# Turning the softmax weights of 320 queries by DMA instead of on TensorE, in a fused attention and Mish MLP kernel

## The chip, the cores and the metric

The kernel runs on one core of a Trainium2 chip. The metric is the device time of one execution, in microseconds. The engines are named as in the profile: PE is TensorE (PEld its weight loads), DVE is VectorE, ACT is ScalarE, POOL is GpSimd, SP is SyncE, which here only issues DMAs.

## The reference, cut to what matters

```python
B, H, S, D = 4, 8, 576, 64                 # batch, heads, queries, head size
q_rot, k_rot = rotate(q), rotate(k)
scores = (1 / sqrt(D)) * q_rot @ k_rot.T
attn = exp(scores - max(scores)); attn = attn / (sum(attn) + 1e-9)
x = (attn @ v)                             # as rows of 8 heads * 64 = 512, 2304 tokens
h = x @ w_in                               # 512 -> 2048
g = h * tanh(log1p(exp(min(h, 20))))       # Mish
out = g @ w_out                            # 2048 -> 512
```

All inputs are fp32. The kernel keeps their accuracy by holding a number as a pair of fp16 values (a high part and the rest), and multiplying pairs in three matmuls: high by high, high by rest, rest by high.

## The kernel before

Two heads make a pair, and four pairs make a batch, so there are 16 pairs, `P` from 0 to 15. Each pair has its 576 queries in steps `step(P, t)`: four steps of 128 queries (`t` 0 to 3), and one step `t` = 4 that takes the last 64 queries of two pairs together. A step is: scores on PE (L505), the maximum on DVE (L513), exp with its sum on ACT (L515), and 1 / sum on DVE (L523, L525). The weights that come out have queries on the partitions, and must be turned, so that keys stand there, before they can be multiplied with V. The turned weights of the first 256 queries of a pair (`k` = 0, steps 0 and 1) and of its last 320 (`k` = 1, steps 2 to 4) go into one tile `et` each, and one call `av(P, k)` multiplies each with V. There are two ways to turn them:

- The exact way keeps fp32. PE transposes the 128 by 128 blocks (L549, L564), sends 1 / sum through a matmul too (L566), ACT or DVE copy the blocks from PSUM to `et` (L558, L559, L573, L575) and 1 / sum to `ew` (L577, L579). `av` is nine fp32 matmuls per half (L636 to L639), and DVE then multiplies with 1 / sum (L667).
- The fp16 way scales the weights to a pair of fp16 values in `ew`: the high part on POOL, ACT or DVE (L530, L532, L533), the rest on DVE (L537). SP issues one DMA transpose for a step (L623), and `av` is 27 fp16 matmuls (L644, L648, L649). V must be there as an fp16 pair, which `cast_v` makes (a load L463, then L466 to L470).

Either way `av` ends with the two halves of `xt`, the fp16 pair of x: its high part (L670, L672) and its rest on DVE (L675). Which way is taken stands in one function, for batch 0 alone:

```python
def exact(P, k):
    return P < NP and (k == 0 or P < NX)
...
    own = exact(P, int(t > 1))
...
    if own:
        turned(es, [(st["ET", p, k], at, t, st["R", p, k], q) for p, k, at, q in to], r)
        return
```

`NP` is 4. The MLP works on 8 blocks of tokens, `c` from 0 to 7: block 2b holds the first 256 queries of batch b, block 2b + 1 its last 320. `h_unit` multiplies with w_in (L883) and takes Mish on ACT (L888), `h_split` makes fp16 pairs (L898, L899, L902), `p_sub` multiplies with w_out (L919). Both weights come as fp32 and are made into fp16 pairs by `decode` (L761 to L781), which needs their largest exponent first: a maximum on DVE (L728), two tiny matmuls on PE and tiny operations on DVE between (L336 to L355). w_out comes in four parts; the loads are L715.

Nothing is scheduled at run time. All operations are recorded in a plan, and the table `ORDER` says in which order they are issued: each entry is an operation's number, with a letter for the engine that takes it where there is a choice, `@` for its PSUM bank, and `+n` for n matmuls without use (L1034, function `fill`) put before it on PE. Every engine works through its own instructions in that order.

Of the kernel before, what the change touches and what calls it, by code (L numbers as in the profile page):

```python
# [50 lines left out]
NX = 2  # L51
# [14 lines left out]
    202 138 105@2 458 162 229@3 184 106 189 34 164 192@2 146 193b 148 144 147 194 208 233 37 185 44 93 35 190 234
    153@1+13 149 165@0 47 51 166 41 235 195 154 236@0 214@54 251b 150 237 49 459 303b 155@1 238 230 209 196 239 107@2
    215 297b 240@0 151 217 216 203 241 152 218 167 285 157@3+6 191 245b 357 270@54 315b 286 158 197 109 108 156 242
    273 159 337@0+5 244@2 48 271 356 250@1 530 219 246 52 274 168 220 287 243 272 247 288@3 252 50 248 169@2 280@4 221
    275 338 53 460 289 170 606 224@0 290 253 257 54 222@3 291 281 276 55 378 292@2 225 322@54 223 293 377 56 256@1  # L70
    278@0 263 581b 462 226@2 277 325 249 279 323 326 282@3 379 461 394 324 380@0 283 294 258 610 341@45+4 228 227 254
    172 381 463 284 339 330@2 296@0 342 373@3 615 331 529 344 231 343 298 259 345 613 299 349@2 262@4 374 332@1 309
    328 260 464 346 327 351@0 347 382 329 350 264 465@3 333 348 383 466 384@2 352 340 353@1 385 375 265 334@3 314@0
    232 266 376 358@54 316 336 267 355 335 386 354 467 302@2 317 454@3 359 308@1 412 468 361 360 400 310 261 362 387
    469@0 311 318 418@54 255 389 455 390 304 456 607 366@1 470 457 305 319 526@3 367 421 411@0 406 171 419 422 546@2
    611 413 420 210 183 414 527 368@4 364 391 423 635@1 212 312b 369b 424 415b 393@5 666@0 268 363 416 471 211 547 395
    636 604@3 396 405@2 619 667 407 399@4 698@1 616 425 408 605 664 401 428@0 409 402 426@3 696 365 269 665 435@54 429
    300b 397 549 370@2 699 398 438 427 783@0 436 439 403b 410b 681@1 371b 404 434 372b 437 800@3 697 433 682 550 612
    511@45 759 472 301 801 818@2 512 57 798 614 755 514 784 430@1 313 641 819 756 760 440 443@3 515 432b 441 822@0 442
    617 445b 431b 213 444b 505 474 446@2 620 513 449@1 499c 447 700 531@54 452 799 306 517 448 388 307 450b 295 820  # L80
    451b 600@3 532 453 826 534 644 533 320 473 535 487 823 516 642 475 536 321 518 476@2 392 523@5 477 757 417 601
    519@1 493 701 478 479 539@2 525b 524b 643 520b 618 480@3 824@4 702 481 482 608b 483 540 537 827 907@0 504@1 821
    825 506 609 498@3 873@5 871 507 908 500 521@2 874 645 501 541@1 602 522 587@45 713 872 542 508b 911 538 603 543@0
    588 509 492@3 830@2 502 545b 544b 494 486@1 503 660@0 495 589 484 590 528 912 637 496b 591 488 497 831 592 717
    622@45 593 575 594 661 489 595 828@3 662 623 703 596b 625 1087@0 829 548 626 743 714 1102 485 551 663 510 598
    552@2 624 553 597 490 646@54+5 638 554 491 628 627 555 629 761 630b 556@1 647 711 1103 631 749b 599 649 648 557
    633 650 632 909 668@54+5 652 651 558 653 559 910 574@3 669 654 634 1130 639 576 655 670 656 1131 568@2 1133@1+5
    657 569b 577 640 658 1147 671 578 570 672 563 571 704 580@0 683@54+4 579 715 572 674 673 562@3 582 1148 573 712
    718 1132 675 564 659 677b 676 780@2 684 705 686 685 565 621 687 583 1175 708 716 566 688 781 719 567b 584 720@3
    721 709 1176 689 560 722 1177 723 690 706 782 724@0 692b 767@54 725 726 679 727 832 737b 1178@3 691b 678 730@1 768  # L90
    731 680 1192 585 770 769 732 771 694 707 785@54 742@2 693 733 835 695 1193 786 734 788 787 735 1232 744 789 772
    790 745 833 748@0 802@54 773 791 561 736@1 774 728 586 750 1233 834 738 746 1235@2 751 776b 836 792 739 775b 815@3
    963 778 740 794b 741b 793b 747b 1249 777 752 850 1234 805 710 1250 753b 806 803 964 875 816 1274 879 817 804 779
    795 837@45 808 854 807 729 809 810b 936@0 838 876 811 754 1275 796 0 877 913@1 881 840 965 839 797 841 966 842 880
    957@3 914 843 812 857@45 844 851 883 845b 915@2 958 860 967 937 846b 813 1036 917@1 916 882 878 861 858 951@3 847
    991 848 859 934 884 1037 894@54 952 862 1276 885 863 953 1039 932@0 1314 864 895 866b 814 897 896 1038 981@2 898
    935 1 918 899 1040 886@3 919@54 1194 887 852 888 849 889 933 868 961@3 983 922 855 959 900 995 1041 1011@1 962 987
    865b 960 985@0 901 996 920 1012 982 903c 902b 867 1030@3 853 984 869 986 921 1032b 890@1 905 1034@2 891 870 1013b
    893 923 1014 1059@0 1031 924 925 904 1042b 938@54 926 1033 1060 954@1 1035 939 928 988 1083b 927b 1195b 940 1084
    1015@3 906 941 992 892 1063@0 942 943 930 1016 929 968@54 764 1196b 931 944 1197 945 946b 1081@2 969 1064 947b  # L100
    1061b 1277@3 971 993 1082 1327 989 949 1108 972 1294 1062 948 1295 970 990 974 950 955b 1085 973 975 998@45 977b
    1086 1315 979 1310 976b 1001 1109 997 999 1002 1078@0 978 1311 1000 1328 1111 980 1017@54 1207 1003 1079b 1004
    1112 1005 1007b 1313@2 1018 1006 856 1020 1019 1104 1110 1149 956 1021 1009 1331 1043@54 1080 1008 1022 1023
    1056@3 1024 1046 1026b 1044 1047 1025c 1312 1028 1355 1045 1010 1105b 1209 1027 1106 1065@45 1113 1049 1107 1048
    1050 1332 1051b 1356 1029 1057 1066 1052b 1150 1058 1067 1068 1370 994 1070 763 1054 1069 1316 1198 1071 1088@45
# [993 lines left out]
```

## Time and profile before

| | us |
|---|---|
| median of 3 runs | 617.98 (616.5 to 618.74) |
| the profiled execution | 618.88 |
| its span in the trace | 616.8 |
| PE busy | 591.1 (96%) |
| DVE busy | 458.0 (74%) |
| ACT busy | 392.1 (64%) |
| POOL busy | 249.5 (40%) |

Busy time is the time in which an engine executes at least one instruction. The fill matmuls count as busy time of PE. The profiled execution took 0.9 us longer than the median.

### The profile page before, as it was taken

Reading aid. Unit: us, or ns where it says so; the run is one execution under the profiler, and the core shown is the slowest. Engines: PE = TensorE matmul, PEld = TensorE weight load, DVE = VectorE, ACT = ScalarE, POOL = GpSimd, SP = SyncE. Lnnn points to the kernel's source line nnn. Section 1 sums busy time; section 2 is a strip of 40 time slices with the busy share of each in tenths; the row PEclk is TensorE's granted clock in tenths of the full one; section 3 lists DMA queues with packets and bytes.
Section 4 is the critical chain, followed back from the end, with each engine's and each line's share of the span. In section 5 each row is a group of like instructions: output and inputs, shape, how many; then the busy total and the mean of one; then the engine's idle time right before and its main releaser. Section 6 shows DMA issues by size and latency. Waiting matters only on the chain.

```text
span 616.8 us, 12860 instructions
## 1 busy us (share of the span) xinstructions
PE 591.1 (96%) x5073; PEld 440.7 (71%) x5073; DVE 458.0 (74%) x964; ACT 392.1 (64%) x767; POOL 249.5 (40%) x222
## 2 busy tenths in 40 slices
PE   5879999989999999999999999999999999999997
PEld 3656676666676665888877767888877778888775
DVE  4989999989899999777789997687787864301130
ACT  3889999976899765687567643766589523521310
POOL 2895676666663546607574313715101100000000
PEclk9999999997999999999999999999999999999999
DMA  9968132495895899836484477534593673200000
GB/s 344 404 250 297 66 135 98 153 202 125 227 261 109 194 232 207 162 81 162 92 219 109 86 138 203 111 77 83 119 126 48 119 135 69 60 1 19 10 20 33
DMA packets 155436, 86.10 MB, mean 140 GB/s; under 512 B 139888, under 2 KB 145648, under 8 KB 153712
## 3 DMA queue, kind: packets, MB, share of 16 engines
q1 hardware_dynamic: 150768, 80.56, 53.4%
q10 hardware_dynamic: 4608, 4.72, 2.4%
q8 instruction: 40, 0.66, 0.4%
q14 instruction: 20, 0.16, 0.1%
HBM read 45.74 MB, written 4.72 MB: 82 GB/s over the span
## 4 chain that ended last, share of the span: by engine, by line
PE 70%; DVE 17%; DMA 5%; ACT 5%; issue 2%; SPq 1%; POOL 0%; DVEq 0%; ACTq 0%
PE bank L883 25%; PE bank L919 24%; PE pair L505 9%; PE bank L648 5%; DVE ew L537 4%; DVE mx L513 4%; PE pair L883 3%; DMA g<-in_w_in 2%; DMA et<-ew 2%; DVE cells L728 1%; PE bank L644 1%; ACT e L515 1%; DVE bank L767 1%; DMA qk<-in_w_out 1%; PE bank L638 1%
## 5 line engine op out<-in xcount | busy, mean ns | idle before, releaser
L919 PEld LDWEIGHTS <-w 128*128 128x128 f16 x1536 | 147.7, 98 | 48.4 <-issue 10.0
L883 PE MATMUL bank<-xt,w 128*128 128x320 f16 (+1 forms) x1380 | 178.3, 286 | 0.0
L883 PEld LDWEIGHTS <-w 128*128 128x128 f16 x1536 | 148.0, 98 | 42.2 <-issue 6.3
L919 PE MATMUL bank<-g,w 128*128 128x320 f16 (+1 forms) x1344 | 175.7, 288 | 0.0
L515 ACT ACTIVATE e<-pair,mx 128x576 f32<-128x576 f32 x144 | 105.8, 739 | 80.6 <-DVE mx L513 58.4
L513 DVE TENSOR_REDUCE mx<-pair 128x1 f32<-128x576 f32 x144 | 104.4, 747 | 23.6 <-PE pair L505 22.5
L537 DVE SCALAR_TENSOR_TENSOR ew<-e,rs,ew 128x576 f16<-128x576 f32 x118 | 117.7, 1010 | 4.5 <-ACT ew L532 4.2
L386 POOL TENSOR_TENSOR raw<-raw,cs 128x576 f32<-128x576 f32 (+2 forms) x61 | 89.7, 1481 | 57.1 <-DMA raw<-in_qk 51.1
L888 ACT ACTIVATE mh<-bank,cells 128x320 f32<-128x320 f32 (+1 forms) x115 | 54.6, 499 | 64.9 <-PE bank L883 57.7
L505 PE MATMUL pair<-qk 64*128 64x288 f32 (+1 forms) x704 | 86.1, 366 | 3.4 <-ACT e L515 2.7
L530 POOL TENSOR_SCALAR ew<-e,rs 128x576 f16<-128x576 f32 x35 | 32.8, 940 | 135.4 <-DVE rs L525 92.5
L505 PEld LDWEIGHTS pair<-qk 64*128 64x128 f32 (+1 forms) x704 | 55.2, 182 | 24.9 <-issue 10.3
L902 DVE SCALAR_TENSOR_TENSOR g<-mh,cells,g 128x640 f16<-128x640 f32 (+1 forms) x56 | 48.6, 877 | 21.8 <-ACT g L898 21.5
L899 DVE TENSOR_SCALAR g<-mh,cells 128x640 f16<-128x640 f32 (+1 forms) x32 | 20.0, 624 | 35.5 <-issue 19.0
L648 PE MATMUL bank<-et,v 128*64 128x320 f16 (+1 forms) x312 | 43.4, 289 | 0.0
L649 PE MATMUL bank<-et,v 128*64 128x320 f16 (+1 forms) x312 | 43.4, 289 | 0.0
L532 ACT ACTIVATE ew<-e,rs 128x576 f16<-128x576 f32 x45 | 34.3, 770 | 12.7 <-issue 6.5
L648 PEld LDWEIGHTS <-v 128*64 128x64 f16 x312 | 32.1, 110 | 9.4 <-issue 6.2
L390 POOL TENSOR_TENSOR raw<-raw 128x288 f32<-128x288 f32 x32 | 35.3, 1116 | 0.5
L649 PEld LDWEIGHTS <-v 128*64 128x64 f16 x312 | 32.1, 110 | 0.0
L523 DVE TENSOR_SCALAR sm<-sm 128x1 f32<-128x1 f32 x144 | 18.6, 144 | 17.4 <-ACT e L515 17.1
L888 ACT ACT_TABLE_LOAD x24 | 30.8, 1283 | 1.0 <-DVE ot L928 0.6
(140 smaller groups left out, 730.5 us busy)
## 6 DMA issues: line engine op xcount, KB each, us to landing
raw<-in_qk SPq DMA_DIRECT2D x30, 576.0 KB, 4.5
w<-in_w_out SPq DMA_DIRECT2D x5, 1024.0 KB, 7.6
g<-in_w_in SPq DMA_DIRECT2D x4, 1024.0 KB, 5.9
w<-in_w_in SPq DMA_DIRECT2D x4, 1024.0 KB, 8.4
stg<-in_v SPq DMA_DIRECT2D x8, 320.0 KB, 4.5
out_dram<-ot ACTq DMA_DIRECT2D x16, 160.0 KB, 2.4
stg<-in_vflat SPq DMA_DIRECT2D x6, 384.0 KB, 3.7
qk<-in_w_out SPq DMA_DIRECT2D x4, 512.0 KB, 6.5
```

What stands on the lines that cost most here:

```text
L386: e.tensor_tensor(out=t()[:, :, s], in0=t()[:, :, s], in1=cs()[:, :, s], op=ALU.mult)
L390: e.tensor_tensor(out=to, in0=t()[:, 0, s], in1=t()[:, 1, s], op=ALU.add)
L505: nc.tensor.matmul(pts[h]()[to, c, :HS], x[own, q], y[own, s], **kw)
L513: op((DVE, dve_ns(S), lambda: nc.vector.tensor_reduce(m(), pt()[:, :, :HS], axis=AX.XY, op=ALU.max, negate=True)), w=[m], r=[pt])
L515: op((ACT, act_ns(S, psum=True, ptr=2) + 35, lambda: nc.scalar.activation(e().rearrange("p (c s) -> p c s", c=2), pt()[:, :, :HS], AF.Exp, ...
L537: op((DVE, dve_ns(S) + 130, lambda: nc.vector.scalar_tensor_tensor(out=w()[:, c], in0=e(), scalar=r()[:, h:h + 1], in1=w()[:, hc], op0=ALU ...
L648: nc.tensor.matmul(po()[0:64, :n], V()[:, vi, c, 0:64], et[:, c, :], start=False, stop=last)
L649: nc.tensor.matmul(po()[64:128, :n], V()[:, vi, c, 64:128], et[:, 5 + c, :], start=False, stop=last)
L883: nc.tensor.matmul(hp(), w1()[:, wi, cc, f:f + 128], x()[:, xi, cc, q0:q0 + n], start=cc == 0 and a == 0, stop=cc == NCC - 1 and a == 2)
L888: op((ACT, act_ns(n, psum=True, ptr=1) + 60, lambda j=j, hp=hp: nc.scalar.activation(hn()[:, j, :n], hp(), AF.Mish, scale=uh())), w=[(hn, ...
L902: op((DVE, dve_ns(2 * n) + 61, lambda: nc.vector.scalar_tensor_tensor(out=gv()[:, 1, f, :n], in0=hn()[:, :, :n], scalar=f32(gs), in1=gv()[ ...
L919: nc.tensor.matmul(pp()[:, :n], w2e[e]()[:, wi, f], gv()[:, gi, f % 4, :n], start=f == 0 and a == 0, stop=f == NF - 1 and a == 2)
```

## The change

`NX` goes from 2 to 0, so `exact(P, 1)` holds for no pair: the last 320 queries of pairs 0 and 1 go the fp16 way, as those of pairs 2 and 3 did before. These are five steps: (0, 2), (0, 3), (1, 2), (1, 3) and the shared step (0, 4). `cast_v` is called for pairs 0 and 1 too. And the table `ORDER` is another one from its first line to its last, since the operations have other numbers and their sequence was chosen anew.

```diff
-NX = 2
+NX = 0
...
 ORDER = """
-    59 2 58 5 3 11 4 6 20 140b 134c 12 111 63 122b 110 128 112 113@0+16 7b 114 115 116 117@1+7 118 13 119 9 127@2 8
...
+    58 2 59 3 11 5 6 4 20 128c 12 110 122c 63 140b 111 134 112 113@2+16 13 114 7b 115 116 117@1+12 118 119 127@0 9
```

By the instructions of the two built programs, the new one has on PE 40 transposes L549 fewer (64 for 104), 10 pairs of matmuls L564 and 10 pairs L566 fewer, two exact `av` of 320 queries fewer and two fp16 ones more, and 42 fill matmuls more (189 for 147). DMA transposes go from 66 to 72, loads of V for `cast_v` from 14 to 16.

The first place where the order matters is DVE in the stretch in which block 0 of the MLP runs and the last 320 queries of batch 0 are attended to. `sm` and `rs` are the sum and 1 / sum of a step, `cells` holds scalars, `e` is exp of the scores, `w` the MLP's weights, `mh` the output of Mish, `xt` and `stg` hold the fp16 pairs made from it there. Before, one exact step and one `av` of 320 queries stand so:

```order
L667 TENSOR_TENSOR ew<-bank_76,ew 128x320
L336 TENSOR_SCALAR cells<-cells 1x1 x2
L579 COPY ew<-pair_78 128x128
L575 COPY et<-pair_78 128x128
L559 COPY et<-bank_74 128x4x128
L355 COPY cells<-bank_76 128x1
```

Now the same engine has at the corresponding place, for the first two of the steps that changed:

```order
L537 SCALAR_TENSOR_TENSOR ew<-e_807,rs,ew 128x576
L902 SCALAR_TENSOR_TENSOR xt_70<-mh,cells,xt_70 128x512
L537 SCALAR_TENSOR_TENSOR ew<-e_811,rs,ew 128x576
L728 TENSOR_REDUCE cells<-qk 128x1
L513 TENSOR_REDUCE mx<-pair_77 128x1
L781 TENSOR_TENSOR w_68<-w_68 128x512
L537 SCALAR_TENSOR_TENSOR ew<-e_864,rs,ew 128x576
L537 SCALAR_TENSOR_TENSOR ew<-e_858,rs,ew 128x576
```

The copies from PSUM are gone, and two L537 per step are there. Up to the eighth L675, which completes x for the last queries of batch 0, DVE has 24 L537 where it had 12.

The second place is the queue of SP, where the last part of w_out is loaded in four pieces (the L715 of 128x512 to `raw` and `qk` below; the L715 to `w_68` is a piece of the part before). Before:

```order
L715 DMA raw<-in_w_out 128x512
L715 DMA w_68<-in_w_out 128x1024
L463 DMA raw<-in_v 128x640
L715 DMA raw<-in_w_out 128x512
L715 DMA qk<-in_w_out 128x512
L623 DMA_TRANSPOSE et<-ew 128x18x128 x2
L623 DMA_TRANSPOSE et<-ew 128x18x64
L380 DMA raw<-in_qk 128x1152
L715 DMA qk<-in_w_out 128x512
```

Now:

```order
L623 DMA_TRANSPOSE et<-ew 128x18x128
L715 DMA w_68<-in_w_out 128x1024
L623 DMA_TRANSPOSE et<-ew 128x18x128
L715 DMA raw<-in_w_out 128x512
L715 DMA qk<-in_w_out 128x512
L623 DMA_TRANSPOSE et<-ew 128x18x128
L715 DMA raw<-in_w_out 128x512
L623 DMA_TRANSPOSE et<-ew 128x18x128
L715 DMA qk<-in_w_out 128x512
```

Before, three of the four pieces stood ahead of every transpose, and the last behind three. Now the first two stand behind six of them, the third behind seven and the last behind eight (four transposes come ahead of the rows shown).

## Rows read from the trace of the kernel before

**Rows 1.** Page, busy time: engine, us, share of the span, instructions.
```profile
PE 591.1 (96%) x5073; PEld 440.7 (71%) x5073; DVE 458.0 (74%) x964; ACT 392.1 (64%) x767; POOL 249.5 (40%) x222
```

**Rows 2.** Windows: stretch, length, busy PE, PEld, DVE, ACT, POOL, clock, DMA.
```profile
0.00:10.00 10.00, 3.72 (x17) 2.30 (x18) 2.93 (x4) 2.68 (x3) 0.88 (x5) 1.00 0.83 305
10.00:72.10 62.10, 53.80 (x417) 36.77 (x416) 58.30 (x146) 52.83 (x120) 47.34 (x46) 1.00 0.75 289
72.10:115.20 43.10, 41.97 (x357) 31.11 (x356) 41.47 (x114) 41.63 (x80) 30.61 (x28) 1.00 0.32 111
115.20:162.50 47.30, 42.77 (x337) 31.00 (x335) 44.25 (x97) 36.71 (x73) 27.36 (x25) 0.93 0.73 171
162.50:254.40 91.90, 90.48 (x732) 60.03 (x731) 85.56 (x163) 70.39 (x136) 54.06 (x46) 1.00 0.89 200
254.40:600.00 345.60, 345.07 (x3124) 270.20 (x3124) 224.36 (x442) 187.38 (x357) 89.24 (x76) 1.00 0.46 96
```

**Rows 3.** Chain that ended last: page by engine, then its pieces from 100 to 170.
```profile
PE 70%; DVE 17%; DMA 5%; ACT 5%; issue 2%; SPq 1%; POOL 0%; DVEq 0%; ACTq 0%
...
125.96 3.07 DVE ew L537 x2
...
131.88 6.24 DMA qk<-in_w_out
138.14 0.69 DVE cells L728
```

**Rows 4.** Waits of DVE from 10 to 162.5 us: total, times, longest.
```profile
DVE cells L728 <- DMA g<-in_w_in: 2.3, 1, 2.3
DVE cells L728 <- DMA qk<-in_w_out: 1.4, 1, 1.4
```

**Rows 5.** Timelines of DVE and PE: start, us; end of batch 0's x, then its use.
```profile
160.29 0.47 DVE L675 SCALAR_TENSOR_TENSOR xt<-bank,xt 128x320 f16<-128x320 f32 x1
...
162.51 5.06 PE L883 MATMUL bank<-xt,w 128*128 128x320 f16 x36
```

**Rows 6.** Lines of PE by form: count, then busy us, mean ns, idle before.
```profile
L549 PE MATMUL bank<-ident,e 128*128 128x128 f32 x92 | 13.7, 281 | 2.3 <-ACT e L515 1.3 <-DVE w L770 0.9
L564 PE MATMUL bank<-ident,e 128*64 128x128 f32 x48 | 5.2, 294 | 0.0
L638 PE MATMUL bank<-et,v 128*64 128x320 f32 x16 | 4.7, 439 | 0.0
L636 PE MATMUL bank<-et,v 128*128 128x320 f32 x4 | 1.5, 459 | 0.0
L648 PE MATMUL bank<-et,v 128*64 128x320 f16 x168 | 25.4, 301 | 0.0
L644 PE MATMUL bank<-et,v 128*128 128x320 f16 x42 | 8.0, 300 | 1.1 <-DMA et<-ew 1.1
L1034 PE MATMUL bank<-ident 128*128 128x256 f16 x98 | 14.5, 300 | 6.0 <-DMA ident<-in_ident 6.0
```

**Rows 7.** Lines of DVE by form, from 10 to 165 us.
```profile
L537 DVE SCALAR_TENSOR_TENSOR ew<-e,rs,ew 128x576 f16<-128x576 f32 x14 | 14.4, 1053 | 0.0
L667 DVE TENSOR_TENSOR ew<-bank,ew 128x320 f32<-128x320 f32 x2 | 0.9, 470 | 0.0
L575 DVE COPY et<-bank 128x128 f32<-128x128 f32 x3 | 0.8, 282 | 0.0
L778 DVE CAST w<-g 128x512 f16<-128x512 f32 x2 | 0.8, 416 | 0.0
L559 DVE COPY et<-bank 128x512 f32<-128x512 f32 x1 | 0.7, 669 | 0.0
```

**Rows 8.** Line L537 from 0 to 165 us: duration ns min/median/max.
```profile
L537 DVE SCALAR_TENSOR_TENSOR ew<-e,rs,ew x14: 796/818/2042, 118.3 to 163.0; 128x576 f16<-128x576 f32 x14
```

**Rows 9.** DMA issues: median us from issue to landing.
```profile
et<-ew SPq DMA_TRANSPOSE x66, 4.7
```

**Rows 10.** Timeline of PE from 136 to 150 us: start, us, idle before.
```profile
139.08 0.27 PE L346 MATMUL bank<-ident,cells 128*1 128x128 f32 x1 [1.57 <-DVE cells L343]
140.50 0.58 PE L352 MATMUL bank<-ident,cells 1*128 1x1 f32 x2 [1.16 <-DVE cells L336]
...
143.24 4.71 PE L919 MATMUL bank<-xt,w 128*128 128x256 f16 x24
```

More of the change, by code (lines that the diff above doesn't have):

```diff
@@ L66 @@
[L66 to L105, printed above, removed]
@@ new lines @@
+    1330 1219 1108 1412 1460@2 1221b 1223 1519@1 1461 1197 1457 1459 1220c 1367 1331@2 1495@3 1332 1493b 1333 1235
+    1464b 1517@2 1515b 1494 1465 1520 1497@0 1222 1496 1518 1236 1368 1251@54 1413 1498 1525@3 1254 1527 1315 1199
+    1252 1237b 1312 1531@1 1255 1264@2 1516 1521b 1245 1253 1526 1523@0 1224 1522 1256 1313 1271@45 1532 1528 1455
+    1551@3 1246 1274 1524 1265 1257 1370 1258 1266 1529@1 1552 757 1204 1260b 1239 1549@3 1238b 1547b 1530 1201 1371
+    1198 1557@0 1249 1240 1550 1259c 1707@1 1275 1553b 1548 1555b 1558 1272 1369 1273 1556 1585 1276 1207 1202 1250b
@@ new lines @@
+    1729 2007 1725 2038@5 1677 2023 2019 2026@0 1746b 1908 2017 1760@3 2015 1827 2024b 1698 2030 1697 2025 1728 1819b
+    2034@2 2031 1761b 2028@1 1730 2035 1678 1731b 2040@2 2039 1733 1679 2027 1762 1747@54 1570 1699 2029 1732c 1669
+    2032@1 1750 2036b 1701c 2046@0 2033 1703 1700b 2042b 2047 2041 1751 2044b 1748 2144@2 2037 1702 2048 1734 1749
+    1704 2045 1777@45 2043 1753 2142@3 1778 1752 1779 1754 1735 1780 1756 2049 1782 1781 1755c 1690 1670 1691 2145
+    1793@45 1757 1862 2143 1904 2104@2 1794 1783 2050b 1795 1758 2052@3 1784 1796 1759 1786 2053 1797 1785c 1788
@@ new lines @@
+    2068 1900b 1920 1821 2166@2 1921 2103 1901 2072 2162@0 1858 1923 1907 1930@45 2147 2168@3 1685 2073b 2163 1922
+    2071 1931 1881 2167 1902 2160@1 1932 1924 1933 2140b 2150@0 1926 1934 1903 1935 1928 2161 2148@2 2141 1925c
+    1948@54 2151 1927 2149 2169 2172@1 1949 1936 1951 1950 1937 2178@2 2164b 1952 2174@3 1953 2165 1954 2173 1955
+    1957c 1968@54 1959 2180@0 1939c 2175 2170b 1829 1938b 2171 1961@1 1868b 2181 1956b 1940 1915 2176b 2069 1971
+    2186@0 2179 1929 1969 1941 1970 2187 2177 2184b 1981@3 1942 1972 1973 1958 1916 2182b 1974 1992@54 1982b 2183 1983
@@ new lines @@
+    2214@2 2234@3 2215 2221 2213 2222@0 2209 2218b 2119 2216@4 2223 2120 2230 2226@0 2217 2224b 2231 2252@5 2135c
+    2136c 2232@4 2137 2219 2238@1 2225 2227 2138 2235 2228@2 2233 2139 2250@3 2229 2239 2236b 2242b 2246@4 2237 2243
+    2244@1 2247 2253 2264@2 2245 2251 2240@5 2152@1 2241 2248 2256 2254 2265 2153b 2154 2255 2258@3 2257 2249 2282@0
+    2259 2283 2260 2266 2298@4 2261 2292@0 2262b 2263 2267 2284@1 2268b 2294@5 2285 2293 2288@1 2295 2286@0 2289
+    2276@2 2277 2270@3 2271 2272 2302 2290b 2269 2303 2273 2278 2274 2287 2300@5 2275 2296b 2291 2279 2297 2301 2299
@@ L165 @@
+    2312@3 2310@1 2304@4 2316@5 2305 2311 2280 2308 2324@1 2313 2320b 2306@4 2321 2322@3 2307 2281 2314b 2309 2318@0
+    2315 2317 2325 2330@2 2323 2319 2328b 2326b 2331 2327 2329 2336@1 2337 2332 2333 2338 2334b 2335 2342@2 2339 2343
+    2340 2341 2348@1 2344 2345 2349 2346b 2347 2350 2351 2352b 2353
 """
```

143 lines of the change are left out of this document (80 added, 63 removed).

## The prediction

> **What bounds the kernel now.** The page's first part comes first: PE is busy 96% of the span, DVE 74% [rows 1]. Read alone, that says that PE bounds everything and that any PE work taken away comes off the time. It is an average over stages, so the windows come next, cut where PE starts another kind of work [rows 2]: at 72.1 us it begins block 0 of the MLP, at 115.2 its second half (L919), at 162.5 block 1, at 254.4 block 2. From 254.4 to 600 PE is idle for 0.5 us of 345.6, and from 162.5 to 254.4 for 1.4 of 91.9: there PE is the bound. Up to 162.5 it is not. PE is idle for 6.3 us of the first 10, 8.3 of the next 62.1, 1.1 of the next 43.1 and 4.5 of the next 47.3, and what it does there holds 147 fill matmuls without use, 21 us at 14.5 / 98 = 0.148 each [rows 6]. In the same stretches DVE is busy 58.3 of 62.1, 41.5 of 43.1 and 44.3 of 47.3 us [rows 2]. ACT is as full as DVE from 72.1 to 115.2 (41.6 of 43.1), but has 10.6 us free from 115.2 to 162.5, where DVE has 3.1.
>
> The chain of waits agrees: PE holds 70% of it, DVE 17%, and DVE's share lies ahead of 162.5; between 100 and 170 its longest links are a load of w_out for 6.2 us and two L537 for 3.1 [rows 3]. Last, the join of the two regimes: the eighth L675, at 160.29 to 160.76, completes x for the last queries of batch 0, and PE starts block 1 on it at 162.51 [rows 5], 1.75 us later, with other work between. Everything behind that point is PE at its limit. So the change is worth what it does to that point, plus what it does to PE's work behind it. By the two programs PE has the same scores, `av` and MLP matmuls behind the point in both, and everything that the change takes from PE lies ahead of it.
>
> **PE's part.** The 40 transposes L549 cost 13.7 / 92 = 0.149 us each, 6.0 us. The 20 matmuls L564 cost 5.2 / 48 = 0.108 each, 2.2 us, and I take the 20 of L566 at the same, 2.2. Two exact `av` of 320 queries cost 4.7 (L638) plus as much for L639, which is alike, plus 1.5 (L636), 10.9 us; two fp16 ones cost 2 / 14 of (25.4 for L648, as much for L649, and 8.0), 8.4 us [rows 6]. PE is relieved of 6.0 + 4.4 + 2.5 = 12.9 us. The 42 new fills give 42 x 0.148 = 6.2 back, so PE is busy for 6.7 us less. All of it lies in the stretch where PE waits, or fills. I cost it at nothing for that reason: its cover is DVE's queue ahead of the eighth L675. If that cover were gone, the 6.7 us would come off the end.
>
> **DVE's part, up to the eighth L675.** Counted in the two programs, priced by their rows [rows 7]:
> - L537 from 12 to 24, at 1.053 us: +12.6.
> - L533 from 0 to 2; taken at 0.5 each, an estimate from the 0.416 of a cast of 512 elements: +1.0.
> - the copies from PSUM: L559, two at 0.669 and two half as wide at some 0.42 (an estimate between 0.282 and 0.669): -2.2. L575 and L579, ten at 0.28 (two of them narrower): -2.7.
> - L667, two at 0.470: -0.9.
> - L778 from 6 to 1, at 0.416, which ACT takes over: -2.1.
> - eleven other kinds that change by one to three instructions: +0.9.
>
> The sum is +6.6 us, on an engine with at most 2 to 3 us free in each of the two stretches. ACT and POOL get more too, but have room: 10.6 and 19.9 us free in the second stretch [rows 2].
>
> **The price of an L537.** This is the term with the widest bounds: in this stage its duration runs from 0.796 to 2.042 us, with a median of 0.818 [rows 8]. If all twelve took the least, they would cost 9.6 us (3.0 less than above); if all took the most, 24.5 (11.9 more). I take the mean, since the new ones stand among the same POOL work. The Trainium skill says why there are two prices (SBUF — State Buffer, "Who interferes with whom"): a DVE instruction with two SBUF inputs, which L537 is, and a GpSimd instruction that reads SBUF want the same port pair, and whoever started first keeps the other out for its whole length. The trace agrees with two prices [rows 8], and cannot say which the new instructions get. By the rule, with every new one blocked, the sum would be +18.5 instead of +6.6.
>
> **DMA's part.** Six more transposes at 4.7 us each from issue to landing [rows 9], beside other DMAs: the engines' share is 0.32 from 72.1 to 115.2 and 0.73 behind it [rows 2], so there is room, and I cost them at nothing while `av` comes some steps later in PE's order. If that cover fails, an `av` waits up to 4.7 us. The Trainium skill speaks against this change here (VectorE: DVE Perf Modes, "The three transpose paths" and "Rules for kernel authors"): it puts a 128 by 128 transpose at 390 ns on TensorE and 1309 ns by DMA, and advises TensorE where PSUM will do as target. A step has 18 such blocks, so by that page one step's transpose would take an estimated 23.6 us, and the last one could end too late. The trace has the whole step landed in 4.7 us [rows 9], so the trace does not bear the page's figure out, and the sum keeps the row.
>
> **The order.** Moved with the rest are the loads of the last part of w_out, now behind six to eight transposes in SP's queue. A transpose waits for its L537 on SP, and the loads behind it wait with it. Before, DVE itself stood still twice for such a load, 2.3 us for w_in and 1.4 us for w_out [rows 4], and PE waited 1.6 and 1.2 us for the exponent of that last part, at 139 and 140 us, after which 24 matmuls L919 took 4.7 us [rows 10] in a stretch whose mean granted clock is 0.93 [rows 2]. The new order may save the 3.7 us of DVE's waits, or repeat them. I take half, -1.8; the ends are 0 and -3.7.
>
> **The sum.** DVE reaches the end of the eighth L675 at 160.76 + 6.6 - 1.8 = 165.6. PE, with less to do, is there earlier, so the 1.75 us between the two is used up, and block 1 starts at about 165.6 for 162.51: +3.1 us. Behind it PE's work is the same and there is nothing to gain. Against the profiled execution that makes 618.88 + 3.1 = 622.0. That execution lies 0.9 us above the median, so I give 621.1.
>
> **Rivals.**
> *Absorbed.* DVE loses both DMA waits (-3.7) and the new L537 come at 0.82 (-2.8): then +6.6 - 6.5 - 1.75 is below zero, PE takes over as the bound at the point, and the time is 616.5 to 619. For it: the median is the low price [rows 8], and the DMA waits [rows 4] are of the order's making. Against it: both have to come together.
> *PE's relief comes through.* If PE and not DVE sets the arrival at block 1, the 6.7 us come off: about 611.3. For it: ahead of 162.5 PE is busy 42.8 of 47.3 us, and waits [rows 10] sit on a chain through PE. It decides if DVE's surplus falls under PE's own saving, so that block 1 starts ahead of 161. Against it: 147 fills and 20 us idle up to that point.
> *A port or a queue makes it dearer.* Either the L537 meet POOL more often (each blocked one +1.2 us over the median), or the last part of w_out comes late, its exponent stops PE in order, and the hole on PE [rows 10] grows by one landing of 4.7 us. For it: three of the four pieces lost their place ahead of all transposes. The time is 624 to 632.
>
> **Numbers.** A measurement of this kernel tells some 0.5%, 3.1 us, from no change: faster is below 614.9, slower above 621.1. My forecast, 619 to 623.5, has 0.50, half of it on each side of the upper bound. Absorbed has 0.21, PE's relief 0.14, dearer 0.15 (0.08 by the port, 0.07 by the queue). So slower 0.25 + 0.15 = 0.40, same 0.25 + 0.21 = 0.46, faster 0.14. The range leaves out PE's relief and the upper part of the dearer case: 615.5 to 627.
>
> **What the profile after would show.** PE's busy time at 584, DVE's some 8 us up. The first L883 with 320 columns at about 165.6 instead of 162.5, right behind the eighth L675; from there to the end the same time as before, within 1 us. Until then DVE busy for 95% from 72 us on, and PE with more fills and idle time. I am wrong if the first such L883 comes at 161 or ahead of it, if PE waits long for an `et` or an exponent ahead of it, or if the time behind it changes by over 2 us, which would be the order's doing and not that of the step that changed.

## The result and the profile after

After takes 626.1 us (625.0 to 626.5), before 617.9 us in the same runs: a ratio of 1.0132, with a 95% interval of 1.0109 to 1.0155, or +8.2 us. The direction was forecast and the size was not: +3.1 us stood in the prediction. The profiled execution of after took 626.52 us, with a span of 624.7.

The page's busy times, and its chain by engine (PE's links in it cannot be followed to the start here, so the shares do not add up to the span):

```profile
PE 584.2 (94%) x5053; PEld 436.9 (70%) x5053; DVE 472.9 (76%) x963; ACT 391.0 (63%) x769; POOL 247.9 (40%) x215
...
PE 57%; DVE 3%; issue 1%; ACT 0%; POOL 0%; DVEq 0%; ACTq 0%
```

PE has 6.9 us less to do than in [rows 1], as forecast (584), and DVE 14.9 us more, where 8 were forecast. The windows of after, cut at the same times as [rows 2] (stretch, length, busy PE, PEld, DVE, ACT, POOL, granted clock, share of the DMA engines, GB/s):

```profile
10.00:72.10 62.10, 50.37 (x380) 34.63 (x380) 57.78 (x139) 49.61 (x113) 50.43 (x47) 0.95 0.79 290
72.10:115.20 43.10, 35.37 (x310) 27.25 (x309) 41.88 (x93) 37.69 (x71) 26.13 (x25) 1.00 0.58 133
115.20:162.50 47.30, 40.98 (x333) 29.15 (x331) 44.54 (x96) 41.09 (x80) 29.60 (x25) 0.96 0.89 188
162.50:254.40 91.90, 87.67 (x718) 58.28 (x717) 87.53 (x166) 69.49 (x134) 49.07 (x39) 1.00 0.91 185
254.40:600.00 345.60, 345.15 (x3150) 270.22 (x3148) 236.36 (x466) 190.58 (x372) 91.82 (x77) 1.00 0.52 105
```

Ahead of 162.5 us DVE is as full as it was and PE has far more holes. The timeline of PE and DVE at the start of block 1, which answers to [rows 5]:

```profile
170.09 1.53 PE L883 MATMUL bank<-xt,w 128*128 128x320 f16 x10
171.94 0.47 DVE L675 SCALAR_TENSOR_TENSOR xt<-bank,xt 128x320 f16<-128x320 f32 x1
172.47 0.70 PE L883 MATMUL bank<-xt,w 128*128 128x320 f16 x4 [0.84 <-DVE xt L675]
```

Block 1 starts at 170.09 us instead of 162.51, +7.6 of the span's +7.9. Behind it nothing changed: 624.7 - 170.1 = 454.6 us to the end, 616.8 - 162.5 = 454.3 before. PE now waits 0.84 us for the eighth L675, which ends at 172.41 and not at 160.76. So the place is the one forecast.

Most of the 7.6 us had arisen much earlier. The first L883, with which block 0 of the MLP begins, in before and in after, and the first L537 of after (each fence is from one kernel's timelines):

```profile
72.14 0.60 PE L883 MATMUL bank<-xt,w 128*128 128x256 f16 x4
```

```profile
77.63 0.61 PE L883 MATMUL bank<-xt,w 128*128 128x256 f16 x4
88.80 1.71 DVE L537 SCALAR_TENSOR_TENSOR ew<-e,rs,ew 128x576 f16<-128x576 f32 x1
```

Block 0 begins 5.5 us late, 11 us ahead of the first of the new L537. From there to block 1 after takes 92.5 us for 90.4, 2.1 more. Of the kinds of work that the new way adds, only casts of V lie ahead of the first L883 (0.5 us on DVE, 1.6 on ACT, 2.8 on POOL; none in before). So, these casts apart, the 5.5 us come with the order. The granted clock was lower there as well, 0.68 from 20 to 30 us where before has 1.00. It is not shown to be the reason: in e7 below it was 0.85 and the first L883 came at 76.6 us, in e4 0.83 from 20 to 40 us and 77.8.

The question is also why DVE gets to the end of the eighth L675 11.7 us later. Lines of DVE up to that moment (0 to 172.41 us; count, busy us, mean ns, idle before):

```profile
L537 DVE SCALAR_TENSOR_TENSOR ew<-e,rs,ew 128x576 f16<-128x576 f32 x24 | 26.9, 1141 | 0.4 <-ACT ew L532 0.4
L390 DVE TENSOR_TENSOR qk<-raw 128x256 f32<-128x256 f32 x2 | 3.3, 1673 | 0.0
L390 DVE TENSOR_TENSOR qk<-raw 128x320 f32<-128x320 f32 x2 | 2.5, 1266 | 0.0
L899 DVE TENSOR_SCALAR stg<-mh,cells 128x512 f16<-128x512 f32 x1 | 1.8, 1757 | 0.0
L667 DVE TENSOR_TENSOR ew<-bank,ew 128x256 f32<-128x256 f32 x4 | 1.6, 405 | 0.0
L533 DVE TENSOR_SCALAR ew<-e,rs 128x576 f16<-128x576 f32 x2 | 1.1, 526 | 0.0
L778 DVE CAST w<-w 128x512 f16<-128x512 f32 x1 | 0.9, 885 | 0.0
```

In before, up to its own eighth L675 (0 to 160.5 us):

```profile
L537 DVE SCALAR_TENSOR_TENSOR ew<-e,rs,ew 128x576 f16<-128x576 f32 x12 | 12.6, 1075 | 0.0
L390 DVE TENSOR_TENSOR qk<-raw 128x320 f32<-128x320 f32 x3 | 1.9, 666 | 0.0
```

L537 went from 12 instructions and 12.6 us to 24 and 26.9, +14.3 where +12.6 stood in the sum. Ten of the twelve more are the five steps' (118 in the whole of before, 128 in after); the other two belong to batch 1 and stand ahead by the new order. L390, the addition of the rotary step, went from three and 1.9 us to four and 5.8, and one L899 of 1.8 us came; both stand in the sum only among the eleven other kinds, at +0.9 together. DVE's waits in the same stretch (total, times, longest):

```profile
DVE cells L348 <- PE bank L346: 2.2, 3, 0.9
DVE cells L355 <- PE bank L352: 2.1, 3, 1.1
DVE mx L513 <- PE pair L505: 1.2, 1, 1.2
DVE cells L728 <- DMA w<-in_w_out: 1.0, 1, 1.0
DVE cells L728 <- DMA g<-in_w_in: 0.7, 1, 0.7
```

The DMA waits of [rows 4] did shrink: L728 waits 1.7 us for loads, 4.7 in before (both counted from 0). But DVE now waits 4.3 us for PE's transposes of the exponents, L346 and L352. Before, L355 waited 0.9 and L348 0.5. Its idle time up to the eighth L675 is 172.41 - 157.29 = 15.1 us, and was 160.76 - 145.62 = 15.1. PE is idle for 32.6 us ahead of block 1, and was for 20.2.

Why is an L390 dear? Timeline of DVE and POOL in after, around one L390 and around three L537 (start, us):

```profile
25.98 2.79 POOL L386 TENSOR_TENSOR raw<-raw,cs 128x512 f32<-128x512 f32 x2
27.47 1.59 DVE L390 TENSOR_TENSOR qk<-raw 128x256 f32<-128x256 f32 x1
...
112.01 1.28 POOL L386 TENSOR_TENSOR raw<-raw,cs 128x512 f32<-128x512 f32 x1 [3.69 <-DMA raw<-in_qk]
112.80 1.10 DVE L537 SCALAR_TENSOR_TENSOR ew<-e,rs,ew 128x576 f16<-128x576 f32 x1
114.25 0.80 DVE L537 SCALAR_TENSOR_TENSOR ew<-e,rs,ew 128x576 f16<-128x576 f32 x1
114.83 1.25 POOL L781 TENSOR_TENSOR w<-w 128x512 f16<-128x512 f32 x1 [1.54 <-ACT w L777]
115.45 1.24 DVE L537 SCALAR_TENSOR_TENSOR ew<-e,rs,ew 128x576 f16<-128x576 f32 x1 [0.40 <-ACT ew L532]
```

The L537 at 114.25 starts when POOL is idle and takes 0.80. The other two start inside an instruction of POOL, which ends at 113.29 and 116.08, and they end at 113.90 and 116.69, in both cases 0.61 us later. The L390 ends at 29.06, 0.29 us behind POOL's L386 (28.77). In these rows such an instruction is not slow; its end comes a fixed time behind the end of POOL's. What it costs is set by where the order puts it.

### The profile page after: what moved, and what is told of

It reads as the page before. It is cut to its first block, busy times and chain, and to the rows that moved or that the text cites. A ratio compares the mean times of both kernels' runs of the same rounds, so it can differ in the third digit from the quotient of the medians.

```text
span 624.7 us, 12838 instructions
## 1 busy us (share of the span) xinstructions
PE 584.2 (94%) x5053; PEld 436.9 (70%) x5053; DVE 472.9 (76%) x963; ACT 391.0 (63%) x769; POOL 247.9 (40%) x215
## 4 chain that ended last, share of the span: by engine, by line
PE 57%; DVE 3%; issue 1%; ACT 0%; POOL 0%; DVEq 0%; ACTq 0%
PE bank L919 23%; PE bank L883 17%; PE pair L505 6%; PE pair L883 4%; PE bank L648 4%; DVE ew L537 2%; PE bank L644 1%; DVE mx L513 1%; DVE ew L533 0%; ACT e L515 0%; DVE ot L928 0%; DVE qk L416 0%; POOL ew L530 0%; PE bank L649 0%; DVE rs L525 0%
## 5 line engine op out<-in xcount | busy, mean ns | idle before, releaser
L919 PEld LDWEIGHTS <-w 128*128 128x128 f16 x1536 | 146.4, 98 | 49.5 <-issue 11.6
L883 PEld LDWEIGHTS <-w 128*128 128x128 f16 x1536 | 148.2, 98 | 46.6 <-issue 10.7
L919 PE MATMUL bank<-g,w 128*128 128x320 f16 (+1 forms) x1344 | 176.6, 288 | 0.8 <-DVE sm L523 0.8
L883 PE MATMUL bank<-xt,w 128*128 128x320 f16 (+1 forms) x1260 | 165.0, 287 | 4.1 <-ACT mh L888 1.6
L515 ACT ACTIVATE e<-pair,mx 128x576 f32<-128x576 f32 x144 | 105.9, 739 | 73.8 <-DVE mx L513 47.6
L537 DVE SCALAR_TENSOR_TENSOR ew<-e,rs,ew 128x576 f16<-128x576 f32 x128 | 132.2, 1047 | 12.1 <-ACT ew L532 9.2
L386 POOL TENSOR_TENSOR raw<-raw,cs 128x576 f32<-128x576 f32 (+2 forms) x62 | 96.0, 1561 | 69.7 <-DMA raw<-in_qk 46.1
L513 DVE TENSOR_REDUCE mx<-pair 128x1 f32<-128x576 f32 x144 | 104.8, 746 | 16.9 <-PE pair L505 16.7
L888 ACT ACTIVATE mh<-bank,cells 128x320 f32<-128x320 f32 (+1 forms) x105 | 49.0, 500 | 50.4 <-PE bank L883 41.9
L530 POOL TENSOR_SCALAR ew<-e,rs 128x576 f16<-128x576 f32 x29 | 26.7, 923 | 112.6 <-DVE rs L525 87.8
L532 ACT ACTIVATE ew<-e,rs 128x576 f16<-128x576 f32 x57 | 43.1, 768 | 17.6 <-DVE rs L525 9.8
L899 DVE TENSOR_SCALAR g<-mh,cells 128x640 f16<-128x640 f32 (+1 forms) x38 | 22.6, 599 | 39.4 <-ACT mh L888 27.0
L649 PE MATMUL bank<-et,v 128*64 128x320 f16 (+1 forms) x336 | 47.1, 290 | 0.0
L648 PE MATMUL bank<-et,v 128*64 128x320 f16 (+1 forms) x336 | 47.0, 290 | 0.0
L1034 PEld LDWEIGHTS <-ident 128*128 128x128 f16 x189 | 19.7, 107 | 24.6 <-issue 14.9
L883 PE MATMUL pair<-xt,w 128*128 128x256 f16 (+1 forms) x276 | 35.7, 282 | 0.0
L928 DVE TENSOR_SCALAR ot<-bank,cells 128x320 f32<-128x320 f32 (+1 forms) x13 | 6.7, 514 | 37.4 <-PE bank L919 37.4
```

The costliest lines, as they stand in the source:

```text
L386: e.tensor_tensor(out=t()[:, :, s], in0=t()[:, :, s], in1=cs()[:, :, s], op=ALU.mult)
L513: op((DVE, dve_ns(S), lambda: nc.vector.tensor_reduce(m(), pt()[:, :, :HS], axis=AX.XY, op=ALU.max, negate=True)), w=[m], r=[pt])
L515: op((ACT, act_ns(S, psum=True, ptr=2) + 35, lambda: nc.scalar.activation(e().rearrange("p (c s) -> p c s", c=2), pt()[:, :, :HS], AF.Exp, ...
L532: (ACT, act_ns(S, ptr=1) + 25, lambda: nc.scalar.activation(w()[:, c], e(), AF.Copy, scale=r()[:, h:h + 1])),
L537: op((DVE, dve_ns(S) + 130, lambda: nc.vector.scalar_tensor_tensor(out=w()[:, c], in0=e(), scalar=r()[:, h:h + 1], in1=w()[:, hc], op0=ALU ...
L648: nc.tensor.matmul(po()[0:64, :n], V()[:, vi, c, 0:64], et[:, c, :], start=False, stop=last)
```

## The experiments

**W** is the theory that the new way costs by DVE's work ahead of block 1. **O** says that the order written for it costs. A third possibility is that PE's time counts. Lines are those of after, shifted by some rows in a kernel with code added. Ratios are to runs of before on the same chip, each with its 95% interval; a us is 0.16% of 617.9.

| run | kernel | ratio to before | interval |
|---|---|---|---|
| | after | 1.0132 | 1.0109 to 1.0155 |
| e1 | new way in before's order | 1.0509 | 1.0464 to 1.0554 |
| e2 | old way in after's order | 1.0396 | 1.0357 to 1.0434 |
| e3 | after, low parts with one input | 1.0090 | 1.0058 to 1.0122 |
| e4 | after, low parts copied | 1.0066 | 1.0039 to 1.0092 |
| e7 | after, L390 copied | 1.0112 | 1.0075 to 1.0148 |
| e8 | after, both copied | 1.0062 | 1.0034 to 1.0091 |
| e6 | before, low parts twice | 1.0123 | 1.0084 to 1.0161 |
| e5 | before, 42 more fills | 1.0093 | 1.0060 to 1.0126 |
| e11 | after, L390 on POOL | 1.0069 | 1.0041 to 1.0098 |
| e12 | e11, low parts copied | 1.0046 | 1.0023 to 1.0069 |
| e16 | before, L390 on POOL | 0.9978 | 0.9960 to 0.9997 |
| e13 | before, order touched up | 0.9995 | 0.9980 to 1.0010 |
| e14 | e11, order touched up | 1.0065 | 1.0043 to 1.0087 |
| e15 | e11, 42 fills fewer | 1.0069 | 1.0046 to 1.0093 |
| e17 | e11, 118 fills more | 1.0096 | 1.0060 to 1.0132 |
| e18 | e16, 60 fills more | 1.0019 | 1.0000 to 1.0039 |
| e9, e10 | both orders searched anew | 1.1595, 1.1583 | 1.1551 to 1.1639, 1.1534 to 1.1632 |

**Way and order exchanged: e1, e2.** Rows that only one way has have no place in the other's order, and were put in by hand (in e1 the low parts and turns where the matmul turns stood).

```diff
 e1, from before, with before's order
-NX = 2
+NX = 0
 e2, from after, with after's order
-NX = 0
+NX = 2
```

> The changed way (weight pairs turned by DMA for the last 320 queries of all four pairs of heads) in the order of before: each new low part and turn stands where the removed matmul turns stood, the two products with the values some 40 rows later, 147 fills as before. Theory W (the way costs: DVE's 12 more low parts L537 at 1.05 to 1.14 us before block 1, less what is removed, +6 to +9 us on DVE's queue): 622 to 627 us, and the first 320-column L883 of block 1 at 166 to 170 us. Theory O (the new order's later first stage costs, the first L883 at 77.6 instead of 72.1 us, and the way is absorbed): 616 to 619 us, first L883 at 72 us. If PE's 12.9 us of removed matmuls came through: below 612 us.

> The order of after, with the last 320 queries of two pairs of heads turned by matmuls again as in before (their turns and evictions put where the exponentials and reciprocals of those steps stand in after's order, 182 fills). Theory W: 616 to 619 us, with the first 320-column L883 near 162 us, since DVE has its 12 low parts back. Theory O: 623 to 627 us, the first L883 of the kernel at 77 us as in after and that of block 1 near 169 us.

Both missed every expectation: 650.8 and 643.6 us. The engines take their instructions strictly in the order, and the rows put in by hand stand where others wait for them. Waits of PE in e1 and of DVE in e2, from 10 to 190 us (their lines are one up and one down from after's):

```profile
PE pair L504 <- ACT e L514: 9.8, 7, 3.6
PE bank L351 <- DVE sm L522: 8.0, 1, 8.0
```

```profile
DVE et L560 <- PE bank L550: 7.8, 3, 5.4
DVE et L576 <- PE bank L567: 7.0, 3, 3.6
```

They tell nothing of way against order, except that the placement of a few rows is worth three to four times what the change is.

**DVE's load taken off after, and put on before: e3, e4, e6, e7, e8.** The edits in the helpers; `one()` and `copy` hold for the last 320 queries of the first two pairs of heads:

```diff
 e3
-nc.vector.scalar_tensor_tensor(out=w()[:, c], in0=e(), scalar=r()[:, h:h + 1], in1=w()[:, hc], ...)
+nc.vector.tensor_scalar(w()[:, c], e(), r()[:, h:h + 1], None, op0=ALU.mult)
 e4, e8
+return nc.vector.tensor_copy(w()[:, c], w()[:, hc])
 e7, e8
+if e is nc.vector:
+    return e.tensor_copy(to, t()[:, 0, s])
 e6 (before; n is 2 for batch 0)
+for _ in range(n):
+    nc.vector.scalar_tensor_tensor(out=w()[:, c], ...)
```

> After, in which the ten low parts L537 of the five steps concerned read one SBUF input instead of two (the low part is then a second copy of the high part: the subtraction is left out), in the same order with the same DMA turns. Theory W: ten times 0.4 to 0.7 us leave DVE's queue ahead of block 1, so 4 to 7 us come back: 619 to 622 us. Theory O, or any theory in which PE or the landing of the turns sets the time: 625 to 627 us, as after.

> After, with the ten low parts of the five steps concerned made by a DVE copy of the fp16 high part (the low part of the weights is left out; order, DMA turns and PE's work unchanged). Estimate from the 1.14 us of an L537 in after: 8 to 9 us leave DVE's queue between 88 us and block 1. Theory W (DVE's queue up to block 1 sets the time): 5 to 8 us come back, 618 to 621 us, first 320-column L883 at 162 to 165 us. Rival O (the order's first stage, already 5.5 us late before any of the ten): at most 2 us, 624 to 626 us.

> Before, in which every low part L537 of batch 0 is computed twice over (the same output, some 12 us more of DVE ahead of block 1 and nothing else). Theory W, DVE's queue sets the arrival at block 1: 626 to 631 us (12 times 1.05 = 12.6 us, less 1.75 us of slack and what idle time DVE had). If DVE has slack there: 617 to 620 us. The share of the 12.6 us that arrives is the price of a us of DVE ahead of block 1, by which the terms of the sum are to be weighed.

> After, with the four L390 on DVE (1.15 to 1.76 us each, where before had three at 0.48 to 1.02 us) made copies of one input (the sum of the rotated halves is left out for them). Some 3 to 5 us leave DVE's queue in the first 40 us. If the lateness of the first stage (first L883 at 77.6 instead of 72.1 us) comes of these dear additions: first L883 at 73 to 75 us and 622 to 624 us. If it comes of PE, ACT or POOL in the new order: first L883 at 77 us still, 625 to 627 us.

> Both of the edits before this one in after: the ten low parts and the four additions made copies. Some 12 to 14 us leave DVE's queue ahead of block 1. Theory W: what before has of it and PE's relief come through, 612 to 617 us, first 320-column L883 at 156 to 161 us. If the two do not add, or another engine takes over: 619 to 623 us.

e6 gave 1.0123, +7.6 us, as W says: DVE's time ahead of block 1 counts in before. It doubles ten L537, not twelve (118 become 128), since the other two of the twelve up to the eighth L675 are batch 1's, and all ten lie ahead of block 1. Up to block 1 DVE is busy for 154.9 us instead of 147.0, and block 1 starts at 168.06, 5.5 us later. Block 2 starts 8.0 us later (262.4 for 254.4). What adds the 2.5 us between the two is not settled: PE waits 1.4 us for an `et` there (1.1 in before), and the granted clock was 0.83 from 240 to 250 us (1.00 in before).

Taking load off after gives back less. e4 took the ten low parts from 11.4 us in all to 5.2 (median 0.30 each, the longest 1.07), and of these 6.2 us 0.66% or 4.1 us came back (some 2.2 either way), short of W's 5 to 8. In its profiled execution, the longest of six, DVE is busy for 5.9 us less up to the eighth L675, and that comes only 1.4 us earlier, at 171.00. DVE's idle time grew from 15.1 to 19.6 us, most of it in waits for PE (0 to 171 us, to be held against the 2.2 and 2.1 us above; lines are shifted):

```profile
DVE cells L348 <- PE bank L346: 4.8, 3, 2.6
DVE cells L355 <- PE bank L352: 2.5, 4, 1.0
```

So DVE's queue alone does not set the time of after. e3, at a mean of 0.86 us each, gave 2.6. e7 gave 1.2 us, which its interval does not tell from nothing, but it tested nothing either, because the copies cost about what the additions had. The line of e7 (duration ns min/median/max, first and last start):

```profile
L391 DVE COPY qk<-raw x4: 987/1260/1630, 13.0 to 39.3; 128x320 f32<-128x320 f32 x2, 128x256 f32<-128x256 f32 x2
```

One input or two, such an instruction waits for POOL. With that, e8 is e4 over again (1.0062), and 612 to 617 us was out of reach.

**PE's load: e5.** Seven fills added at each of six rows of before, as here:

```diff
-    ... 526@3 367 ...
+    ... 526@3+7 367 ...
```

> Before, with 42 more fill matmuls in six places between the first L883 and the first L919 (six times seven, 6.2 us of PE's time at the 0.149 us of one, by the rows of before). The step of the prediction under test is that PE's time ahead of block 1 is hidden: then 617 to 620 us. If PE's time there counts in full: 623 to 625 us; in between, the share of PE's time that counts.

1.0093, +5.8 us for 6.2 us of PE: the 617 to 620 us of hidden fills were missed. But the profiled execution does not put the loss ahead of block 1. Windows of e5 at its own first L883, first L919 and block 1:

```profile
73.90:120.00 46.10, 45.12 (x392) 34.11 (x390) 40.71 (x112) 41.64 (x78) 29.77 (x28) 1.00 0.30 103
120.00:164.40 44.40, 40.02 (x337) 29.73 (x335) 42.29 (x97) 36.45 (x73) 26.87 (x24) 1.00 0.81 176
164.40:259.90 95.50, 92.56 (x733) 60.55 (x733) 85.43 (x164) 70.48 (x136) 55.70 (x46) 0.98 0.93 196
```

The first L883 comes 1.7 us later than in before, ahead of every added fill. The stretch with the fills is 3.0 us longer than in [rows 2], and PE is busy in it for 45.1 of 46.1 us. The next stretch is 2.9 us shorter, so that block 1 starts only 1.9 us late. Another 3.6 us come between block 1 and block 2, where PE waits for a transpose twice as long as in before (1.1 us):

```profile
243.59 0.98 PE L644 MATMUL bank<-et,v 128*128 128x320 f16 x3 [2.36 <-DMA et<-ew]
```

The granted clock did not fall between 140 and 150 us (0.66 there in before), but from 40 to 50 (0.66) and from 240 to 250 (0.83). So PE's time costs in the stretch where the fills stand, and the program is slower with them; that it costs at block 1, as the step under test has it, is not shown.

**The additions to POOL: e11, with its control e16, and e12.** In the order, letters give the engine; four rows of after change theirs (three of before in e16):

```diff
-    14 10 ... 24b ... 40b
+    14b 10b ... 24 ... 40
```

> After, with its four L390 on DVE (5.8 us of DVE's time, most of it behind POOL's instructions) given to POOL, at their places in the order; nothing else moves and nothing is left out. If the dear additions on DVE are a term of the 8.2 us: 2 to 4 us come back, 621.5 to 624 us, first L883 at 74 to 76 us. If POOL, now with four more, or PE sets the first stage: 625 to 628 us.

> Before, with its three L390 on DVE (1.9 us in all) given to POOL, the control for e11. If the 3.9 us that e11 gave back are the dear additions of after's order (5.8 us for four, each behind an instruction of POOL): no gain here, 616.5 to 620 us. If POOL is simply the better place: 2 us or more less than before.

> After, with its four L390 given to POOL (as in the run e11) and the ten low parts of the five steps concerned copied from the high part (as in e4: the low part is left out). If the two terms that stand for half of the loss each (3.9 and 4.1 us by those runs) are separate terms of one queue, they add: 617 to 620 us, the time of before, first 320-column L883 at 161 to 163 us. If one took the other's gain: 622 to 624 us.

e11 gave back 1.0132 - 1.0069 = 0.63% (the two intervals together leave some 0.37% either way), 3.9 us, with nothing left out: up to the eighth L675 DVE is busy for 151.2 us instead of 157.3. In the profiled execution, at 621.74 us 2.3 below e11's median, the first L883 came at 74.0 us for 77.6, and block 1 here:

```profile
165.19 1.53 PE L883 MATMUL bank<-xt,w 128*128 128x320 f16 x10
```

In before the same edit gave 1.4 us (some 1.1 either way): its three additions cost 1.9 us, not 5.8. So by the medians 2.5 us of the gain belong to where after's order puts them, though the intervals together leave as much either way. With the same edit in both, the two kernels are 1.0069 - 0.9978 = 0.91% apart, 5.6 us (some 2.1 either way). e12 came to 1.0046, 1.4 us under e11 (some 2.3 either way) where e4 alone had 4.1: by the medians the two terms do not add, and the intervals do not settle it. In e12's profiled execution block 1 starts where it does in before:

```profile
162.43 0.85 PE L890 MATMUL bank<-xt,w 128*128 128x320 f16 x5
```

and that execution took 619.09 us, but it was the fastest of ten (619.1 to 625.1). By the medians 2.8 us are left.

**Both orders searched: e9, e10, then e13, e14.** e9 and e10 have wholly new orders. e13 moves 54 rows of before, and e14 60 rows of e11, and these operations change their engine:

```diff
 e9, the first rows
-    59 2 58 5 3 11 4 6 20 140b 134c 12
+    58 110 59 111 134 3 11 112 2 113@2+16 114 122
...
 e13, from before
-    134c 14 581b 453 567b 753b 845b 2359b
+    134b 14b 581 453b 567 753 845 2359
 e14, from e11
-    122c 128c 7b 8b 16b 49 407b 396b 1637b 2352b
+    122 128b 7 8 16 49b 407 396 1637 2352
```

> The kernel before (two pairs' last 320 queries turned by matmuls), with its order searched anew: rows, engines of an operation and PSUM banks moved by a search whose durations are those of the two traces, and in which a DVE instruction of the kind that POOL holds up (L537, L533, L902, L899, L390) waits for the end of POOL's instruction. The work is the same. If the order as it stands leaves time on the table: 603 to 613 us, with the first 320-column L883 at 146 to 156 instead of 162.5 us. If the search only fits the model: 616 to 622 us.

> After (all four pairs by DMA), with its order searched in the same manner and for as long. Theory W (the way costs by its DVE work, +3 to +6 us, whatever the order): 3 to 6 us over the re-ordered kernel of before, 606 to 616 us. Theory O (the way is about neutral, and after's order is the worse of the two orders): within 2 us of it. If the way itself is what costs 8 us: 8 us or more over it.

> The kernel before with 54 rows of its order moved by at most 12 places at a time and 8 operations given to another engine, each for a gain by the durations of the traces, with ACT's table loads counted (1.28 us each, which the search before this one left out: 91 of them in place of 47 is a large part of what those two orders lost). By those durations 6 us: 609 to 616 us. If the order as it stands is at its best: 616 to 622 us.

> After with the four L390 on POOL, and its order touched up in the same manner and for as long (60 rows moved, 10 operations given to another engine). Theory O (after's order, not its way, holds most of the 8 us): within 3 us of the touched-up kernel of before, 609 to 618 us. Theory W (the way's DVE work costs, whatever the order): 5 us or more over it, 617 to 622 us.

The first two took 718.2 and 717.5 us. Lines of ACT in e9:

```profile
L888 ACT ACT_TABLE_LOAD x46 | 59.0, 1283 | 0.8
L515 ACT ACT_TABLE_LOAD x45 | 57.7, 1283 | 11.4 <-DVE ew L537 7.1 <-DVE mx L513 3.1 <-DVE sm L523 0.5
```

The search had moved Mish (L888) and exponentials (L515) between each other, and each change of function loads ACT's table for 1.28 us: 91 loads, where before has 47. In e9 the 44 loads more are 56 us of ACT, of 98 us lost; the rest is not explained. With the loads counted, the touched-up before came out as before (0.9995) and the touched-up after as e11 (1.0065). The promised gains were not there, so both orders are about as good as these moves make them. Between the two stand 0.70%, 4.3 us (some 1.7 either way), more than O's 3 and less than W's 5: the pair settles for neither. In the profiled executions most of the distance lies ahead of the new low parts: the first L883 comes at 76.5 us in e14 and at 72.1 in e13, block 1 at 166.2 and 159.7, so 4.4 of 6.5 us are there before e14's first L537 starts at 85.9.

**Fills in the new way: e15, e17, e18.** Only the numbers behind the plus signs change, at seven rows in e15 and at many in e17 and e18, for instance:

```diff
 e15
-    467@1+20 815@5+11
+    467@1+5 815@5
 e17
-    691@3 776@0
+    691@3+6 776@0+6
```

> After with the four L390 on POOL (as e11), and with 42 of the fill matmuls between 60 and 131 us taken out, so that it has 147 as before (6.2 us of PE's time). If PE's time ahead of block 1 is hidden, as the prediction has it: 622 to 625 us, as e11. If it counts, as the run with 42 more fills in before says: 617 to 621 us. If the fills pay by the clock that they hold up: 625 us or more, with a lower granted clock ahead of block 1.

> After with the four L390 on POOL (as e11) and 118 more fill matmuls, each put where PE waits in the traces between 12 and 165 us for longer than the fill takes (307 in all, where e15 has 147 and e11 189). In the profiled executions of e11, e15 and the copies the granted clock fell in some slices ahead of 165 us, each time behind a hole on PE, and the time varied from 620.8 to 627.5 us from one execution of e11 to the next. If the clock's falls are what is left of the loss: granted clock 1.00 from 10 us on, 618 to 621 us with little spread. If PE's time counts, or the fills meet the wrong holes: 625 to 630 us.

> Before with its three L390 on POOL (as e16) and 60 more fill matmuls, each put where PE waits by the same rule (207 in all). The clock of before fell once, to 0.66 from 140 to 150 us. If that fall is worth what its slice shows (some 3 us): 614 to 617 us, the fastest of the kernels here. If not: 617 to 620 us, as e16. A gain here and in e17 alike is the clock's and speaks for neither way.

e15 equals e11 (1.0069 both, some 2.3 us either way): taking 6.2 us of fills off PE gives nothing. Whether PE's time was hidden or went into a lower clock is not separated. Its profiled execution was the longest of nine, 628.8 us, and these windows show a lower granted clock than e11's profiled execution had in the same stretches (0.98 and 1.00):

```profile
0.00:74.00 74.00, 56.79 (x406) 38.06 (x408) 58.97 (x142) 53.65 (x118) 54.65 (x57) 0.93 0.78 285
74.00:113.50 39.50, 30.89 (x240) 22.66 (x238) 38.72 (x88) 33.59 (x62) 24.85 (x23) 0.87 0.56 142
```

e17 and e18 put fills into PE's holes instead, and lost 1.7 and 2.5 us to e11 and e16, e17's loss within its interval. e18's granted clock did not fall anywhere up to 170 us in the profiled execution, and block 1 started at 160.6 us, but the time was no shorter than before's. Between block 1 and block 2 it lost more than that: PE waited for a transpose here too, the granted clock was 0.74 from 240 to 250 us, and block 2 started at 257.3 us for 254.4.

```profile
240.09 0.98 PE L644 MATMUL bank<-et,v 128*128 128x320 f16 x3 [2.35 <-DMA et<-ew]
```

So the clock's falls ahead of block 1 are not shown to be what is left.

## Why the size was wrong, step by step

- **Everything behind block 1's start is PE at its limit, so the change is worth what it does to that start.** Right for this change: +7.6 of +7.9 us of the span. It does not hold for a gain. In their profiled executions e13, e16 and e18 start block 1 2.8, 1.3 and 1.9 us ahead of before, and their spans are 616.6, 618.5 and 619.9 us for 616.8.
- **PE's part, 6.7 us less, worth nothing.** Right in the new way as far as e15 tells (PE 6.9 us less; the 147 fills are 21.8 us by their price, not 21). The sentence it rested on, that up to 162.5 us PE is not the bound, is too wide: from 72.1 to 115.2 PE was busy for 41.97 of 43.1 us [rows 2], and the fills that e5 adds there lengthen that stretch by 3.0 us. More load was charged on either engine (e6, e5), and less did not pay back in full (4.1 of 6.2 us in e4, none in e15).
- **DVE's part, +6.6 us.** This is the step that failed: it came to 11.7. The terms that the change names were L537 +14.3 (12.6), L533 +1.1 (1.0), L559 -2.2 (-2.2), L575 and L579 -2.7 (-2.7), L667 -0.9 (-0.9), L778 -1.6 (-2.1), together +7.9 for 5.7. The rest, "eleven other kinds that change by one to three instructions: +0.9", came to +3.8, with L390 at +3.9, L899 at +1.8 and the others at -1.9. I counted instructions and priced them by before's means, although the new order also changes what POOL does beside them. e11 takes L390's 5.8 us off DVE and gets 3.9 back, where e16 takes off 1.9 and gets 1.4. And the prediction looked for the loss where the five steps are: 5.5 of the 7.6 us at block 1 were there by the first L883.
- **The price of an L537.** 1.141 us each for the 24, for 1.053, so that risk came in at 1.7 us. The trace does not have two prices but a low one, 0.80 to 0.82, and any above it up to 2.09, by how long POOL still ran. What I said of it holds for more lines: L390 has two SBUF inputs too. The Trainium skill (SBUF — State Buffer, "Who interferes with whom") says that copies, casts and one-input scalar instructions of DVE can contend with GpSimd as well, and the trace agrees: 1.76 us for the L899, 0.885 for a cast of 0.416 [rows 7], 0.99 to 1.63 for e7's copies.
- **The order, -1.8 us.** Failed too: 3.0 us of DVE's waits for loads went, and 2.9 of waits for PE's L346 and L352 came. Nothing was left.
- **DMA's part, nothing.** Right: the six `et` of the stretch from 80 to 125 us landed in 3.9 to 10.0 us (median 6.1, [rows 9]: 4.7), and PE has no wait for one there. The estimated 23.6 us from the Trainium skill's figure did not show (VectorE: DVE Perf Modes, "The three transpose paths").

Sum with the measured terms: 160.76 + 11.7 + 0 = 172.4, the measured end of the eighth L675. This is bookkeeping of one execution, in which DVE's idle time happens to be the same; it does not say which of the 11.7 us would come back (e4). Block 1 itself starts 2.3 us ahead of that, at 170.09, on columns that were ready. PE is not there earlier, as the sum had it: it works without a break from 161.08 us to 171.62.

Of the rivals, the dearer port came true in part, by L390 (+3.9 us) more than by L537 (+1.7); the late load of w_out did not; PE's relief did not come through. Of the 8.2 us, 3.9 came off with L390 on POOL (1.4 by the same edit in before). Between the two ways stand 5.6 us with that edit in both (e11, e16) and 4.3 with both orders touched up (e13, e14), whose interval holds the 3.1 of the forecast. Copying the low parts on top takes 1.4, within its interval. The rest has no cause that a run showed. By the profiles of e13 and e14 most of it lies ahead of the first L883, so it is not the new low parts' time alone.

## What to carry

In a schedule with in-order queues, count what an edit does to *every* instruction that moves, and price each by what the engine beside it does at that moment; a mean over another order hides it. Do not read relief and load alike: 6 us of fills more cost 5.8 in one kernel here, and 6 us fewer gave nothing in another. Follow a delay from one join to the next before naming its cause: here most of it stood ahead of the step that changed. A changed step put by hand into another order is no control; changing four letters, or one helper, is.
